# Moving a branch's key-value step behind the first denominators, with single weight loads and paired last heads, in a gated linear-attention kernel

## The chip, the cores and the metric

The kernel runs on one core of a Trainium2 chip. The metric is device time in microseconds (us) of one execution. Before the change it was 190.77 us (median of three runs, 190.71 to 191.03). A run's time is some 1.3 us longer than the span that the profile shows (for instance 191.05 against 189.7 in the profiled run of the kernel before), so spans are compared with spans and times with times.

Two sorts of numbers are used below. Times and ratios come from timed rounds. Everything inside a run comes from one profiled execution of each kernel.

## The reference, cut to what matters

Two linear-attention blocks, A and B, read the same x (2048 x 640) with their own weights, and a gate mixes them.

```python
x = A_x                                             # 1 x 2048 x 640, bf16
g = sigmoid((x * gate_w).sum(-1, keepdims=True))
def block(x, wqkv, wo):                             # H = 32 heads, Dh = 20
    q, k, v = split(x @ wqkv)
    phi = lambda t: where(t > 0, t + 1, exp(t)) + 1e-6
    pq, pk = phi(q), phi(k)
    kv  = einsum("bhsd,bhse->bhde", pk, v)          # 20 x 20 for each head
    z   = pk.sum over s
    num = einsum("bhqd,bhde->bhqe", pq, kv)
    den = einsum("bhqd,bhd->bhq", pq, z) + 1e-6
    return merge_heads(num / den) @ wo
out = g * block(x, A_wqkv, A_wo) + (1 - g) * block(x, B_wqkv, B_wo)
```

## The kernel before

The kernel never forms v for all positions. It forms G = phi(k)ᵀx, multiplies it by wv to get the kv of every head, and folds kv into wo: W' = blockdiag(kv) @ wo, 640 x 640 for each branch. The output is then (phi(q) / den) @ W' for A and for B, mixed by the gate.

A list scheduler inside the kernel receives operations in program order, each with an engine, an estimated duration and the buffers it reads and writes. It decides their order on each engine by simulated start time, and among operations that could start within 20 ns of each other by priority, which is program order. TensorE runs, in order: keys of A and B, the G products, the queries in blocks 0 to 3 (ten query units for each block, each five matmuls of 512 columns), and the finals, the matmuls that give the output. The denominators of two blocks are computed together. Their reciprocals, called the factor below, go through DRAM to come back in the layout of the queries (`RX`), and VectorE multiplies the queries by them.

A query unit also costs ScalarE an exponential, and VectorE two operations. The second of these is a max-add that reads the PSUM bank, and only then is the bank free for a later matmul.

```python
        def q_unit(X, b, k):
            # ... five matmuls into one PSUM bank (tile) ...
            # ACT : ek = exp(tile)
            # DVE : ek = min(ek, 1) + EPS
            # DVE : PQ[X][:, k, block b] = max(tile, 0) + ek        ("max-add", frees the bank)
```

The key-value step of a branch (`m_unit`) is a run of small matmuls, tiled to 64 columns of the array, two of them side by side. The last two heads have no partner and run one at a time. VectorE then copies the results into `MB` under a block-diagonal mask: two large masks (60 x 300) and a small one (40 x 40).

```python
        def m_unit(X):
            tile = _Tile(1)
            last = XS.index(X)
            def steps():
                r = []
                for q in range(6):
                    w = 12 if q < 5 else 8
                    for j in range(NC):
                        for g in (0, 1) if q < 5 else (last,):        # the last heads: one side only
                            at = D * j + 120 * q + 60 * g * (q < 5)
                            r.append((PS[64 * g : 64 * g + 64, ...], WV[X][:, at : at + 64], GT[X][...], j == 0, j == NC - 1, (0, 64 * g)))
                return r
            mms("m%s" % X, steps, [("GT", X, k) for k in range(NC)] + [("WV", X), ("WVP", X)], [(tile,)], 25 * 75 + 400)
            for q0, q1, g, w in ((0, 5, 0, 12), (0, 5, 1, 12), (5, 6, last, 8)):
                # ... DVE: MB[...] = PS[...] * mask ...
```

Six W' units follow (`wp_unit`: two matmuls of 320 columns, evicted to `WS`). `WS` is stored to DRAM and read back in another row order into `WPA` or `WPB` (`wp_store`, `wp_rows`). The finals of a branch need those rows.

```python
        def queries(b):
            for X in XS:
                for k in range(NC):
                    q_unit(X, b, k)
                    q = 5 * (X == "B") + k - WPLAG                    # WPLAG = 2
                    if b == 1 and 0 <= q < 6:
                        wp_unit("B", (q - 1) % 6)                     # the six W' units of B lie in block 1
                        if q == 0:
                            wp_rows("A")
        # ...
        queries(0)
        m_unit("B")
        queries(1)
        wp_store("B")
        wp_rows("B")
        d01 = dens(0)             # denominators of blocks 0 and 1: tiled to 32 columns
        scale_q(0, d01, 2)        # DVE: reciprocal; factor through DRAM; DVE: multiply the queries
        queries(2)
        queries(3)
        scale_q(1, d01, 2)
        d23 = dens(2)
        finals(0)
        # ... scale_q and finals of the other blocks ...
```

At the start, the key weights of A come in single chunks of 128 rows on two issuing queues, SP and ScalarE. Those of B come in three loads of one, two and two chunks, all on SP.

```python
        load_x("SP", 0);  load_wk("ACT", 0);  load_x("SP", 1);  load_wk("ACT", 1)
        load_wk("SP", 2); load_wk("ACT", 3);  load_wk("SP", 4)
        for c0, c1 in ((0, 1), (1, 3), (3, 5)):
            dma("SP", "wkB%d" % c0, WK["B"][:, c0:c1, :], weights("B", D, c0, c1), ...)
```

## Time and profile before

| | before |
|---|---|
| time, median | 190.77 us |
| span in the profile | 189.7 us |
| TensorE busy | 98% |
| VectorE busy | 69% |
| first 512-column matmul (end of the start) | 11.30 us |
| from there to the end ("body") | 178.44 us |

The page of the kernel before opens with the span and the busy time of each engine (share of the span, number of instructions). Its fourth part gives the chain of work that ended last.

```profile
span 189.7 us, 3209 instructions
...
PE 186.3 (98%) x1289; PEld 124.0 (65%) x1289; DVE 130.1 (69%) x275; ACT 76.4 (40%) x129; POOL 8.2 (4%) x14
...
PE 94%; DMA 3%; SPq 1%; DVE 0%; issue 0%; DVEq 0%
```

TensorE (PE) is the chain for 94% of the span, so a microsecond taken off PE counts, and so does a microsecond in which PE is made to wait. The 3% of DMA is the weight load at the start.

The table of stretches of the kernel before gives the busy time of each engine in a window. The first window is block 1 of the queries, the second blocks 2 and 3 after the denominators.

```profile
core 0: us, PE busy (x) PEld busy (x) DVE busy (x) ACT busy (x) POOL busy (x), PEclk, DMA share, GB/s
...
107.30:122.00 14.70, 14.70 (x77) 8.54 (x76) 12.72 (x26) 10.14 (x17) 0.00 (x0) 1.00 0.33 99
...
124.50:147.00 22.50, 22.50 (x119) 12.81 (x121) 22.13 (x45) 11.62 (x20) 0.00 (x0) 1.00 0.27 84
```

VectorE (DVE) has 2 us to spare in block 1 (12.72 of 14.70), where B's masks lie now. In blocks 2 and 3 it has almost none (22.13 of 22.50). An average over the whole span (69%) hides this.

The timeline of the kernel before, cut to the operations that the change moves (start, duration, engine, line, operation, count, and in brackets the idle time before it with its releaser). L383 is the helper that records every matmul, so matmuls are told apart by their tiles:

```profile
9.39 2.94 PE L383 MATMUL ps<-WK,XT 128*128 128x320 bf16 x18 [0.24 <-DMA WK<-in_B_wqkv_dram]
...
106.20 1.13 PE L383 MATMUL ps<-GTB,WVB 128*64 128x60 bf16 x55
...
107.36 1.02 DVE L647 TENSOR_TENSOR MB<-ps,CB 60x300 bf16<-60x300 f32 x1
...
117.30 0.44 PE L383 MATMUL ps<-WOB,MB 124*120 124x320 bf16 x2
...
118.72 0.34 SPq L372 DMA_DIRECT2D wrowsB<-WS  x1
...
123.72 0.35 SPq L372 DMA_DIRECT2D WPB<-wrowsB  x1
123.81 1.75 DVE L793 RECIPROCAL RC<-DN 128x256 bf16<-128x256 f32 x1
```

The wait at 9.39 us is the last that PE has. The key-value step of B runs at 106.20 us, its first large mask at 107.36, its last W' unit at 117.30. The rows are stored at 118.72, and their load is issued at 123.72 and lands at 127.91 (read from the trace). The first final of B uses them at 144.00.

### The profile page before, as it was taken

Reading aid. Unit: us, or ns where it says so; the run is one execution under the profiler, and the core shown is the slowest. Engines: PE = TensorE matmul, PEld = TensorE weight load, DVE = VectorE, ACT = ScalarE, POOL = GpSimd, SP = SyncE. Lnnn points to the kernel's source line nnn. Section 1 sums busy time; section 2 is a strip of 40 time slices with the busy share of each in tenths; the row PEclk is TensorE's granted clock in tenths of the full one; section 3 lists DMA queues with packets and bytes.
Section 4 is the critical chain, followed back from the end, with each engine's and each line's share of the span. In section 5 each row is a group of like instructions: output and inputs, shape, how many; then the busy total and the mean of one; then the engine's idle time right before and its main releaser. Section 6 shows DMA issues by size and latency. Waiting matters only on the chain.

```text
span 189.7 us, 3209 instructions
## 1 busy us (share of the span) xinstructions
PE 186.3 (98%) x1289; PEld 124.0 (65%) x1289; DVE 130.1 (69%) x275; ACT 76.4 (40%) x129; POOL 8.2 (4%) x14
## 2 busy tenths in 40 slices
PE   8999999999999999999999999999999999999995
PEld 3565555555788888888855666455556677777774
DVE  1398989898600009996179997899999959833324
ACT  2255555555311112203255478565553522331332
POOL 8900000000000000000000000000000000000000
DMA  6999699991011111112144004665000173211212
GB/s 184 282 229 202 183 381 371 352 241 43 0 35 38 35 35 38 35 35 38 35 86 111 5 22 173 165 223 171 0 0 3 43 228 92 97 66 46 73 69 69
DMA packets 31936, 21.49 MB, mean 113 GB/s; under 512 B 16818, under 2 KB 31666, under 8 KB 31922
## 3 DMA queue, kind: packets, MB, share of 16 engines
q1 hardware_dynamic: 31490, 20.80, 39.4%
q10 hardware_dynamic: 432, 0.49, 0.8%
q8 instruction: 10, 0.16, 0.4%
q14 instruction: 4, 0.03, 0.1%
HBM read 12.05 MB, written 5.31 MB: 91 GB/s over the span
## 4 chain that ended last, share of the span: by engine, by line
PE 94%; DMA 3%; SPq 1%; DVE 0%; issue 0%; DVEq 0%
PE ps L383 94%; DMA WK<-in_B_wqkv_dram 3%; SPq L372 1%; DVE OL L862 0%; DVEq L276 0%
## 5 line engine op out<-in xcount | busy, mean ns | idle before, releaser
L383 PE MATMUL ps<-WK,XT 128*128 128x512 bf16 (+2 forms) x250 | 44.1, 337 | 0.4 <-DMA WK<-in_B_wqkv_dram 0.2
L383 PE MATMUL ps<-XN,FE 128*128 128x320 bf16 x320 | 44.3, 300 | 0.0
L383 PEld LDWEIGHTS ps<-XN,FE 128*128 128x128 bf16 x320 | 37.5, 117 | 6.0
L383 PEld LDWEIGHTS ps<-WK,XT 128*128 128x128 bf16 x250 | 24.0, 98 | 20.2 <-DMA WK<-in_B_wqkv_dram 1.1
L743 ACT ACTIVATE EK<-ps 128x512 bf16<-128x512 f32 x40 | 23.9, 597 | 18.4 <-PE ps L383 17.4
L563 ACT ACTIVATE EK<-ps 128x512 bf16<-128x512 f32 (+1 forms) x42 | 21.4, 526 | 16.2 <-PE ps L383 16.2
L752 DVE SCALAR_TENSOR_TENSOR FE<-ps,EK 128x512 bf16<-128x512 f32 x40 | 26.8, 688 | 0.7
L856 ACT ACTIVATE TS<-ps,GA 128x640 f32<-128x640 f32 (+2 forms) x18 | 13.1, 735 | 29.3 <-PE ps L383 29.3
L383 PE MATMUL ps<-WPB,FE 128*128 128x320 bf16 (+1 forms) x165 | 24.5, 295 | 0.0
L383 PE MATMUL ps<-WPA,FE 128*128 128x320 bf16 (+1 forms) x165 | 24.5, 295 | 0.0
L573 DVE SCALAR_TENSOR_TENSOR FE<-ps,EK 128x512 bf16<-128x512 f32 (+1 forms) x42 | 23.9, 597 | 0.5
L862 DVE SCALAR_TENSOR_TENSOR OS<-ps,GA,TS 128x640 bf16<-128x640 f32 x15 | 13.0, 870 | 15.2 <-PE ps L383 15.2
L383 PE MATMUL ps<-XT,WQA 128*128 128x512 bf16 x100 | 22.8, 380 | 0.0
L383 PE MATMUL ps<-XT,WQB 128*128 128x512 bf16 x100 | 22.7, 379 | 0.0
L600 ACT ACTIVATE GS<-ps 128x640 bf16<-128x640 f32 x10 | 7.0, 704 | 37.0 <-PE ps L383 37.0
L383 PEld LDWEIGHTS ps<-WPA,FE 128*128 128x128 bf16 x165 | 16.0, 98 | 6.2
L383 PEld LDWEIGHTS ps<-WPB,FE 128*128 128x128 bf16 x165 | 15.8, 98 | 6.2 <-ACT TS L856 0.4
L383 PEld LDWEIGHTS ps<-XT,WQB 128*128 128x128 bf16 x100 | 11.7, 117 | 9.2
L383 PEld LDWEIGHTS ps<-XT,WQA 128*128 128x128 bf16 x100 | 11.6, 118 | 9.4 <-issue 0.4
L705 DVE SCALAR_TENSOR_TENSOR GP<-XN,GWB 128x640 bf16<-128x640 bf16 x16 | 13.3, 828 | 4.1 <-PE ps L383 3.6
L567 DVE TENSOR_SCALAR EK<-EK 128x512 bf16<-128x512 bf16 (+1 forms) x42 | 11.4, 272 | 3.1
L811 DVE TENSOR_TENSOR FE<-FE,RX 128x1280 bf16<-128x1280 bf16 (+1 forms) x20 | 12.6, 686 | 0.9 <-DMA RX<-factor 0.9
(52 smaller groups left out, 80.8 us busy)
## 6 DMA issues: line engine op xcount, KB each, us to landing
out_dram<-OS SPq DMA_DIRECT2D x15, 160.0 KB, 1.8
XN<-in_A_x_dram SPq DMA_DIRECT2D x3, 640.0 KB, 8.4
factor<-RC SPq DMA_DIRECT2D x4, 256.0 KB, 2.6
RX<-factor SPq DMA_DIRECT2D x4, 256.0 KB, 3.0
WVA<-in_A_wqkv_dram SPq DMA_DIRECT2D x1, 800.0 KB, 10.8
WQA<-in_A_wqkv_dram SPq DMA_DIRECT2D x1, 800.0 KB, 12.2
WVB<-in_B_wqkv_dram SPq DMA_DIRECT2D x1, 800.0 KB, 11.2
WQB<-in_B_wqkv_dram SPq DMA_DIRECT2D x1, 800.0 KB, 12.2
```

Of the source, the lines that this page charges most:

```text
L372: ins = e.dma_start(dst() if callable(dst) else dst, src() if callable(src) else src, transpose=transpose)
L383: ins = pe.matmul(o, l, r, start=a, stop=z, tile_position=tp, skip_group_check=True)
L563: "ACT", lambda e, ps=ps, ek=ek: e.activation(ek(), ps(), ACT.Exp), _act_ns(n), reads=[(tile,)], writes=[(es,)],
L567: "DVE", lambda e, ek=ek: e.tensor_scalar(ek(), ek(), 1.0, EPS, op0=ALU.min, op1=ALU.add), _dve_ns(n, 4),
L573: return e.scalar_tensor_tensor(out=out, in0=two(ps()), scalar=0.0, in1=two(ek()), op0=ALU.max, op1=ALU.add)
L600: "ACT", lambda e: e.activation(GS[:, k, :].rearrange("p (h f) -> p h f", f=HALF), pair(tile, HALF), ACT.Copy),
L705: lambda e, t=t: e.scalar_tensor_tensor(out=GP[:, :], in0=XN[:, t, 0:D], scalar=1.0, in1=GWB[:, :], op0=ALU.mult, op1=ALU.mult, accum_out= ...
L743: "ACT", lambda e: e.activation(ek(), PS[:, tile.banks[0], :], ACT.Exp), _act_ns(512), reads=[(tile,)],
L752: lambda e: e.scalar_tensor_tensor(out=dst, in0=PS[:, tile.banks[0], :], scalar=0.0, in1=ek(), op0=ALU.max, op1=ALU.add),
L811: return e.tensor_tensor(out=v, in0=v, in1=RX[:, xs.slot, 512 * x + w * j : 512 * x + w * j + w].unsqueeze(1).to_broadcast([128, NC, w]), ...
L856: "ACT", lambda e: e.activation(t_ap(), acc(), ACT.Copy, scale=GA[:, 0, t : t + 1]), _act_ns(hi - lo),
L862: lambda e: e.scalar_tensor_tensor(out=o_ap(), in0=acc(), scalar=GA[:, 1, t : t + 1], in1=t_ap(), op0=ALU.mult, op1=ALU.add),
```

## The change

The intent is to take a few tenths of a microsecond off TensorE. The last heads of A and B run side by side. The key-value step goes directly behind the denominators, so one change of the array's tiling mode falls away. The weights of B arrive in single chunks, so the last bytes hold up fewer matmuls. The W' units of B then have to move from block 1 into blocks 2 and 3.

```diff
-WPLAG = 2
+WPAT = (25, 26, 27, 29, 30, 31)
@@ loads @@
-        for c0, c1 in ((0, 1), (1, 3), (3, 5)):
-            dma(
-                "SP", "wkB%d" % c0, WK["B"][:, c0:c1, :], weights("B", D, c0, c1), ...
-            )
+        for c in range(NC):
+            load_wk(("SP", "ACT")[c % 2], "B", c)
@@ m_unit (cut) @@
-        def m_unit(X):
-            tile = _Tile(1)
+        def m_unit(X, after=None):
+            tiles = [_Tile(1)] + [_Tile(1)] * (X == "B")
             def steps():
+                r = [step(X, tiles[0], q, g, j) for q in range(5) for j in range(NC) for g in (0, 1)]
+                if X == "B":
+                    r += [step(Y, tiles[1 - g], 5, g, j) for j in range(NC) for g, Y in enumerate(XS)]
                 return r
+            parts = [(0, 0, 5, 0, 12), (0, 0, 5, 1, 12)]
+            if X == "B":
+                parts = [(1, 5, 6, 0, 8), (0, 5, 6, 1, 8)] + parts      # two small masks, then two large ones
@@ dens / scale_q (cut): the two copies of the denominators move from scale_q into dens @@
@@ queries @@
-                    q = 5 * (X == "B") + k - WPLAG
-                    if b == 1 and 0 <= q < 6:
-                        wp_unit("B", (q - 1) % 6)
-                        if q == 0:
+                    p = 10 * b + 5 * (X == "B") + k
+                    if p in WPAT:
+                        i = WPAT.index(p)
+                        wp_unit("B", (i - 1) % 6)
+                        if i == 0:
                             wp_rows("A")
+                        if i == 5:
+                            wp_store("B")
+                            wp_rows("B")
@@ order at the end @@
         queries(0)
-        m_unit("B")
         queries(1)
-        wp_store("B")
-        wp_rows("B")
-        d01 = dens(0)
-        scale_q(0, d01, 2)
+        d0, d1 = dens(0)
+        m_unit("B", den[0])
         queries(2)
+        scale_q(0, d0, 2)
         queries(3)
-        scale_q(1, d01, 2)
-        d23 = dens(2)
+        scale_q(1, d1, 2)
+        d2, d3 = dens(2)
```

A number in `WPAT` counts query units from the first of block 0, so 25 is the sixth unit of block 2 and 31 the second of block 3.

More of the change, by code (lines that the diff above doesn't have):

```diff
@@ L409, in load_x, with load_wk @@
             dma(eng, "xn%d" % t, XN[:, t, 0:D], xin[128 * t : 128 * t + 128, :], writes=[("XN", t)], us=0.25)
-        def load_wk(eng, c):
-            dma(eng, "wkA%d" % c, WK["A"][:, c, :], weights("A", D, c, c + 1)[:, 0, :], writes=[("WK", "A", c)], us=0.25)
+        def load_wk(eng, X, c):
+            dma(eng, "wk%s%d" % (X, c), WK[X][:, c, :], weights(X, D, c, c + 1)[:, 0, :], writes=[("WK", X, c)], us=0.25)
         load_x("SP", 0)
-        load_wk("ACT", 0)
+        load_wk("ACT", "A", 0)
         load_x("SP", 1)
-        load_wk("ACT", 1)
-        load_wk("SP", 2)
-        load_wk("ACT", 3)
-        load_wk("SP", 4)
-        for c0, c1 in ((0, 1), (1, 3), (3, 5)):
-            dma(
-                "SP", "wkB%d" % c0, WK["B"][:, c0:c1, :], weights("B", D, c0, c1), writes=[("WK", "B", c) for c in range(c0, c1)],
-                us=0.55 * (c1 - c0),
-            )
+        load_wk("ACT", "A", 1)
+        load_wk("SP", "A", 2)
+        load_wk("ACT", "A", 3)
+        load_wk("SP", "A", 4)
+        for c in range(NC):
+            load_wk(("SP", "ACT")[c % 2], "B", c)
         for t0, t1 in ((2, 4), (4, 8), (8, 12), (12, 16)):
@@ L620, in zbd @@
             )
-        def m_unit(X):
-            tile = _Tile(1)
-            last = XS.index(X)
-            def steps():
-                r = []
-                for q in range(6):
-                    w = 12 if q < 5 else 8
-                    for j in range(NC):
-                        for g in (0, 1) if q < 5 else (last,):
-                            at = D * j + 120 * q + 60 * g * (q < 5)
-                            r.append((
-                                PS[64 * g : 64 * g + 64, tile.banks[0], 60 * q : 60 * q + NC * w], WV[X][:, at : at + 64],
-                                GT[X][:, j, :, 24 * q + 12 * g * (q < 5) : 24 * q + 12 * g * (q < 5) + w], j == 0, j == NC - 1, (0, 64 * g),
-                            ))
-                return r
-            mms("m%s" % X, steps, [("GT", X, k) for k in range(NC)] + [("WV", X), ("WVP", X)], [(tile,)], 25 * 75 + 400)
-            for q0, q1, g, w in ((0, 5, 0, 12), (0, 5, 1, 12), (5, 6, last, 8)):
+        den = {}
@@ new lines, in m_unit, with step @@
+        def m_unit(X, after=None):
+            tiles = [_Tile(1)] + [_Tile(1)] * (X == "B")
+            def step(Y, tile, q, g, j):
+                w, lo = (12, 12 * g) if q < 5 else (8, 0)
+                at = D * j + 120 * q + DH * lo // 4
+                return (
+                    PS[64 * g : 64 * g + 64, tile.banks[0], 60 * q : 60 * q + NC * w], WV[Y][:, at : at + 64],
+                    GT[Y][:, j, :, 24 * q + lo : 24 * q + lo + w], j == 0, j == NC - 1, (0, 64 * g),
+                )
+            def steps():
+                r = [step(X, tiles[0], q, g, j) for q in range(5) for j in range(NC) for g in (0, 1)]
+                if X == "B":
+                    r += [step(Y, tiles[1 - g], 5, g, j) for j in range(NC) for g, Y in enumerate(XS)]
+                return r
+            ys = XS if X == "B" else ("A",)
+            mms(
+                "m%s" % X, steps, [("GT", Y, k) for Y in ys for k in range(NC)] + [("WV", Y) for Y in ys] + [("WVP", Y) for Y in ys],
+                [(t,) for t in tiles], (len(tiles) + 9) * 190 + 240, after=after,
+            )
+            parts = [(0, 0, 5, 0, 12), (0, 0, 5, 1, 12)]
+            if X == "B":
+                parts = [(1, 5, 6, 0, 8), (0, 5, 6, 1, 8)] + parts
+            for i, q0, q1, g, w in parts:
@@ L642, in m_unit, with mask @@
                 n = DH * (w // 4)
-                def mask(e, q0=q0, q1=q1, g=g, w=w, n=n):
+                def mask(e, i=i, q0=q0, q1=q1, g=g, w=w, n=n):
                     p0 = 64 * g
@@ L648, in mask @@
                         out=MB[p0 : p0 + n, q0:q1, 60 * g : 60 * g + n].rearrange("p q (i k) -> p q k i", k=NC),
-                        in0=PS[p0 : p0 + n, tile.banks[0], 60 * q0 : 60 * q0 + n * (q1 - q0)].rearrange("p (q k i) -> p q k i", k=NC, i=w),
+                        in0=PS[p0 : p0 + n, tiles[i].banks[0], 60 * q0 : 60 * q0 + n * (q1 - q0)].rearrange(
+                            "p (q k i) -> p q k i", k=NC, i=w
+                        ),
                         in1=m.unsqueeze(1).to_broadcast([n, q1 - q0, NC, w]), op=ALU.mult,
@@ L653, in m_unit @@
                 sch.op(
-                    "DVE", mask, _dve_ns(n * (q1 - q0)), reads=[(tile,), ("CB",)], writes=[("M", q) for q in range(q0, q1)],
+                    "DVE", mask, _dve_ns(n * (q1 - q0)), reads=[(tiles[i],), ("CB",)], writes=[("M", q) for q in range(q0, q1)],
                     name="mm%s" % X,
@@ L760, in dens, with steps @@
             dtile = _Tile(1)
-            def den():
+            def steps():
                 r = []
@@ L773, in den, with scale_q @@
                 return r
-            mms(
-                "den%d" % b0, den, [("ZBD", X) for X in XS] + [("PQ", X, k, b) for X in XS for k in range(NC) for b in (b0, b0 + 1)],
+            den[b0] = mms(
+                "den%d" % b0, steps, [("ZBD", X) for X in XS] + [("PQ", X, k, b) for X in XS for k in range(NC) for b in (b0, b0 + 1)],
                 [(dtile,)], 5 * 540,
             )
-            return dtile
-        def scale_q(b, dtile, pieces):
-            ds = _Tile(1, ring["dn"])
-            lo = 256 * (b % 2)
-            sch.op(
-                "ACT",
-                lambda e: e.activation(DN[:, ds.slot, :], PS[:, dtile.banks[0], lo : lo + 256], ACT.Identity, bias=EP[:, 0:1]), _act_ns(256),
-                reads=[(dtile,), ("EP",)], writes=[(ds,)], name="dn%d" % b,
-            )
+            ds = []
+            for b in (b0, b0 + 1):
+                d = _Tile(1, ring["dn"])
+                ds.append(d)
+                sch.op(
+                    "ACT",
+                    lambda e, d=d, lo=256 * (b - b0): e.activation(
+                        DN[:, d.slot, :], PS[:, dtile.banks[0], lo : lo + 256], ACT.Identity, bias=EP[:, 0:1]
+                    ),
+                    _act_ns(256), reads=[(dtile,), ("EP",)], writes=[(d,)], name="dn%d" % b,
+                )
+            return ds
+        def scale_q(b, ds, pieces):
             def rec(e):
@@ L936, in bass_gated_mix__linear_attn_block__linear_attn_block__prompt_kernel @@
         queries(0)
-        m_unit("B")
         queries(1)
-        wp_store("B")
-        wp_rows("B")
-        d01 = dens(0)
-        scale_q(0, d01, 2)
+        d0, d1 = dens(0)
+        m_unit("B", den[0])
         queries(2)
+        scale_q(0, d0, 2)
         queries(3)
-        scale_q(1, d01, 2)
-        d23 = dens(2)
+        scale_q(1, d1, 2)
+        d2, d3 = dens(2)
         finals(0)
-        scale_q(2, d23, 2)
+        scale_q(2, d2, 2)
         finals(1)
-        scale_q(3, d23, 4)
+        scale_q(3, d3, 4)
         finals(2)
```

## The prediction

> **What bounds the kernel now.** The page shows TensorE (PE) busy 98% of 189.7 us; the chain of waits is PE for 94%, with 3% for the load of the second wk at the start. From 9.39 us to the last matmul PE never waits. But VectorE (DVE) is as full where blocks 2 and 3 of the queries run: the table of stretches gives DVE 22.13 of 22.50 us from 124.5 to 147.0, and only 12.7 of 14.7 us in block 1 before it.
>
> **What the change does, on PE (starts read in the timeline).**
> 1. Start. The last four matmuls of the first B tile wait until 9.39 us for a two-chunk load. With single chunks only two should wait for the last chunk: estimate 0.27 us saved (two matmuls at 136 ns), if the last byte lands when it did.
> 2. Last heads in pairs. An unpaired 64x40 matmul takes 32 ns, a pair too. The A step loses its five: 0.16 us saved.
> 3. B key-value step behind the denominators. Entering a column-tiled stretch costs 309 ns instead of 216, leaving it about 0.1 us. The Trainium skill (TensorEngine Tiling (Array Packing), Key Properties) says that changing the tiling mode drains the array; the trace agrees with these 0.1 us. One such change fewer: 0.1 to 0.2 us saved.
>
> Sum: about 0.6 us less PE work.
>
> **What it moves.** The four B masks (two of 1.02 us, two of 0.29) and the six W' units leave block 1, where DVE had room, and go behind the two reciprocals (1.75 us each) in block 2, where it has none. From the first denominator matmul (T), with durations of the trace: denominators copied T+1.8, reciprocals and small masks to about T+5.4, the two large masks with one query step between them to about T+8.4. PE's own work to the first W' unit that needs them (denominators 1.1, key-value 1.1, five queries at 1.08, one unit 0.27) ends at about T+7.9. So PE waits about 0.5 us there, then about 0.6 us for the next query unit, whose bank frees only when DVE has caught up (that query's max-add, about T+9.2 to 9.6). These waits swallow saving 3.
>
> **Second new wait.** In the trace, 10.6 us pass from the last W' unit of B to its rows being back (store 4.9, load 4.2, both by DMA). Before, the rows were back 14 us before need. After, only eight query units and the first A half of the final lie between: 8 x 1.08 + 1.36 + 0.27 = 10.3 us; ScalarE also evicts a query first. Estimate: PE waits 0.5 us at the first final of B.
>
> **Prediction.** -0.6 + 1.1 + 0.5 = about +0.9 us; PE is the chain, so all of it counts: 191.5 us, 8 in 10 between 190.3 and 192.5. Faster by over 2%: 0.01; within 2%: 0.97; slower: 0.02.
>
> **What would show it.** Right: the first 512-column matmuls start about 0.3 us earlier; the denominators start near 118.8 us, not 122.0; the waits list PE on DVE masks or max-adds around 126 to 128 us, and PE on the DMA of the B rows near 143; finals begin near 143, not 142.6. Wrong: no PE idle in blocks 2 and 3.
>
> **What would make it wrong.** If consecutive masks overlap more on DVE than I took, the first waits halve. If the rows come back faster on the quiet queue, the second wait vanishes: then 190.2. If the extra loads on ScalarE's queue delay the first branch's chunks, step 1 gives nothing.

## The result, and the profile after

| | before | after |
|---|---|---|
| time, median of six runs (range) | 190.74 us (190.50 to 191.07) | 192.83 us (192.47 to 193.68) |
| ratio after to before (95% interval) | | 1.0116 (1.0092 to 1.0141) |
| span in the profile | 189.7 us | 192.0 us |
| first 512-column matmul (after: see below) | 11.30 us | 11.60 us |
| body (span less the line above) | 178.44 us | 180.44 us |

The kernel got slower by 2.1 us. That is within 2%, as predicted, but the time lies above the predicted range of 190.3 to 192.5 us.

The page of the kernel after, the same parts:

```profile
span 192.0 us, 3199 instructions
...
PE 186.4 (97%) x1279; PEld 124.0 (65%) x1289; DVE 130.7 (68%) x275; ACT 76.5 (40%) x129; POOL 8.1 (4%) x14
...
PE 83%; DMA 8%; DVE 5%; SPq 1%; ACT 1%; issue 1%; DVEq 0%; ACTq 0%
```

PE falls from 94% of the chain to 83%; DMA and VectorE take its place. The counts need care. PE shows 1279 matmuls and 1289 weight loads. Ten matmul records are missing from this trace, so a missing 216 ns is taken for a wait only where the weight load is late too. The record of the first 512-column matmul is among the missing ones in every trace but that of the kernel before; its start is put one ordinary distance (216 ns) before the second's, where its weight load stands too. The same holds for busy time: it did not fall although work was taken away. All PE waits of this document are therefore measured from the starts of successive matmuls in the trace, less the ordinary distance (216 ns for 512 columns, 136 ns for 320). The waits view gives somewhat less, because the ends of matmuls are modelled.

What TensorE waited for in the kernel after (total us, times, longest us):

```profile
...
PE ps L383 <- DVE FE L760: 0.7, 1, 0.7
PE ps L383 <- DVE MB L653: 0.6, 1, 0.6
PE ps L383 <- DMA WPB<-wrowsB: 0.4, 1, 0.4
...
```

These are the new waits that the prediction named: a mask (MB), a max-add (FE), and the rows of B (WPB). By the starts of matmuls they are 0.72, 0.87 and 0.61 us.

The table of stretches of the kernel after, for the window in which masks, W' units and queries of blocks 2 and 3 now lie together:

```profile
122.00:144.30 22.30, 20.93 (x99) 11.71 (x100) 22.11 (x43) 13.83 (x23) 0.00 (x0) 1.00 0.49 142
```

VectorE is full again (22.11 of 22.30), and now PE is not (20.93). How the 1.6 us of the first two waits arise is seen in the timeline of VectorE in the kernel after, from the denominators on. They started at 119.30 us.

```profile
121.12 1.75 DVE L804 RECIPROCAL RC<-DN 128x256 bf16<-128x256 f32 x1
122.79 0.20 DVE L653 TENSOR_TENSOR MB<-ps,CB 40x40 bf16<-40x40 f32 x1
122.84 1.73 DVE L804 RECIPROCAL RC<-DN 128x256 bf16<-128x256 f32 x1
124.61 0.29 DVE L653 TENSOR_TENSOR MB<-ps,CB 40x40 bf16<-40x40 f32 x1
124.92 0.29 DVE L755 TENSOR_SCALAR EK<-EK 128x512 bf16<-128x512 bf16 x1
125.25 1.02 DVE L653 TENSOR_TENSOR MB<-ps,CB 60x300 bf16<-60x300 f32 x1
126.03 0.75 DVE L760 SCALAR_TENSOR_TENSOR FE<-ps,EK 128x512 bf16<-128x512 f32 x1
126.81 1.02 DVE L653 TENSOR_TENSOR MB<-ps,CB 60x300 bf16<-60x300 f32 x1
127.86 0.49 DVE L755 TENSOR_SCALAR EK<-EK 128x512 bf16<-128x512 bf16 x2
128.39 1.29 DVE L760 SCALAR_TENSOR_TENSOR FE<-ps,EK 128x512 bf16<-128x512 f32 x2
```

The scheduler put the second reciprocal between the small masks, and the large ones came last. The last large mask ends at 127.83, and the timeline of PE shows the two consequences:

```profile
127.98 0.45 PE L383 MATMUL ps<-WOB,MB 124*120 124x320 bf16 x2 [0.56 <-DVE MB L653]
...
129.14 0.41 PE L383 MATMUL ps<-XT,WQB 128*128 128x512 bf16 x1 [0.70 <-DVE FE L760]
```

The first W' unit that needs the large masks could have started at 127.26. The query unit behind it needs a bank that a max-add frees at about 129.09.

The chain of the kernel after shows the third wait, with the round trip of the rows (start, duration, what):

```profile
136.19 0.61 ACT WS L690
136.81 4.91 DMA wrowsB<-WS
...
141.79 4.43 DMA WPB<-wrowsB
146.22 0.05 issue
146.27 43.27 PE ps L383 x335
```

What answers to the wait at 9.39 us of before, in the timeline of the weight loads of PE (PEld) at the start:

```profile
6.69 0.39 PEld L383 LDWEIGHTS ps<-WK,XT 128*128 128x128 bf16 x4 [0.47 <-DMA WK<-in_A_wqkv_dram]
...
7.53 0.93 PEld L383 LDWEIGHTS ps<-WK,XT 128*128 128x128 bf16 x8 [0.45 <-DMA WK<-in_A_wqkv_dram]
...
9.41 2.50 PEld L383 LDWEIGHTS ps<-WK,XT 128*128 128x128 bf16 x19 [0.41 <-DMA WK<-in_B_wqkv_dram]
```

PE now waits twice for weights of A, where it waited once before (0.4 us). The two waits end with the third and fourth of A's five chunks, which landed (arrived in SBUF) at 6.65 and 7.48 us, against 5.69 and 6.71 before. The last chunk of A landed at 7.71 us against 7.10 before, and the last of B at 9.75 against 9.35.

The bookkeeping of the body is then: +0.72 +0.87 (mask and query unit) +0.61 (rows) −0.15 (five unpaired matmuls fewer) −0.13 (one change of mode fewer) = +1.92 us, of 2.00 measured (180.44 less 178.44). The start adds 0.29 in this pair of profiles.

### The profile page after: what moved, and what is told of

Read it like the earlier page. It is cut to its first block, busy times and chain, and to the rows that moved or that the text cites. A ratio compares the mean times of both kernels' runs of the same rounds, so it can differ in the third digit from the quotient of the medians.

```text
span 192.0 us, 3199 instructions
## 1 busy us (share of the span) xinstructions
PE 186.4 (97%) x1279; PEld 124.0 (65%) x1289; DVE 130.7 (68%) x275; ACT 76.5 (40%) x129; POOL 8.1 (4%) x14
## 3 DMA queue, kind: packets, MB, share of 16 engines
HBM read 12.05 MB, written 5.31 MB: 90 GB/s over the span
## 4 chain that ended last, share of the span: by engine, by line
PE 83%; DMA 8%; DVE 5%; SPq 1%; ACT 1%; issue 1%; DVEq 0%; ACTq 0%
PE ps L383 83%; DMA WK<-in_B_wqkv_dram 3%; DMA wrowsB<-WS 3%; DMA WPB<-wrowsB 2%; DVE RC L804 2%; DVE MB L653 1%; SPq L372 1%; DVE FE L760 1%; ACT EK L751 1%; DVE EK L755 1%; DVE OL L873 0%; ACT WS L690 0%; DVEq L276 0%; SPq L274 0%; ACTq L276 0%
## 5 line engine op out<-in xcount | busy, mean ns | idle before, releaser
L383 PE MATMUL ps<-XT,WQA 128*128 128x512 bf16 x95 | 21.8, 379 | 0.4 <-issue 0.2
```

The source lines that it names most:

```text
L383: ins = pe.matmul(o, l, r, start=a, stop=z, tile_position=tp, skip_group_check=True)
```

## The experiments

Fourteen kernels ran, in four groups. Each was correct, with six timed runs (four for the repeat of the changed kernel). The theory is that the loss has three parts: the order of work on VectorE, the late rows, and the start's loads. Its rivals are that VectorE's load itself makes PE wait, whatever the order; that the paired heads or the tiling cost time; and that the start only varies from run to run and the loads don't matter.

Landing times and starts are from one profile each:

| kernel | loads of B's weights | last chunk of A lands | first 512-column matmul | body | ratio to before (95%) |
|---|---|---|---|---|---|
| before | old | 7.10 | 11.30 | 178.44 | |
| after | two queues | 7.71 | 11.60 | 180.44 | 1.0116 |
| start_two_queues | two queues | 8.65 | 12.15 | 178.46 | 1.0011 (0.9986 to 1.0035) |
| start_one_queue | single, one queue | 6.89 | 11.03 | 178.46 | 0.9994 (0.9970 to 1.0018) |
| old_loads | old | 6.52 | 10.78 | 180.07 | 1.0088 (1.0067 to 1.0110) |
| late_recip | old | 6.71 | 11.12 | 179.04 | 1.0029 (1.0008 to 1.0050) |
| early_w | old | 6.98 | 11.20 | 179.80 | 1.0068 (1.0052 to 1.0083) |
| all_three | old | 6.61 | 10.70 | 178.89 | 1.0067 (1.0035 to 1.0099) |
| all_three_one_queue | single, one queue | 7.78 | 11.56 | 179.68 | 1.0038 (1.0007 to 1.0069) |
| after_again | two queues | 7.79 | 11.83 | 180.38 | 1.0129 (1.0113 to 1.0146) |
| order_and_room | old | 6.20 | 10.44 | 178.68 | 1.0011 (0.9994 to 1.0029) |
| order_and_room_two | two queues | 8.58 | 12.05 | 178.71 | 1.0045 (1.0026 to 1.0065) |
| order_and_room_one | single, one queue | 6.32 | 10.62 | 178.70 | 0.9986 (0.9971 to 1.0000) |
| pairs_only | old | 6.23 | 10.92 | 178.28 | 0.9982 (0.9966 to 0.9998) |
| pairs_one_queue | single, one queue | 7.34 | 11.03 | 178.31 | 1.0007 (0.9989 to 1.0025) |
| pairs_two_queues | two queues | 8.07 | 11.69 | 178.31 | 1.0020 (0.9994 to 1.0045) |

### The start alone: the change's loads, and the same chunks on one queue

Both edits are made to the kernel before.

```diff
 # start_two_queues
+        for c in range(NC):
+            dma(("SP", "ACT")[c % 2], "wkB%d" % c, WK["B"][:, c, :], weights("B", D, c, c + 1)[:, 0, :], ...)
 # start_one_queue
+        for c in range(NC):
+            dma("SP", "wkB%d" % c, WK["B"][:, c, :], weights("B", D, c, c + 1)[:, 0, :], ...)
```

> The kernel before, with only the start of the change: the five wk chunks of the second branch one by one, alternately on SyncE's and ScalarE's queue. Theory (the extra loads on ScalarE's queue take DMA time from the first branch's chunks, so every chunk lands later): 0.2 to 0.4 us slower than before, first 512-column matmul near 11.6 us against 11.30, and a new wait of TensorE for a chunk of the FIRST branch's wk longer than the 0.2 us it has before. Rival 1, the prediction's step 1 (single chunks save two matmuls' wait): 0.27 us faster, first 512-column matmul near 11.0. Rival 2 (the start of the changed kernel's profile was chance of one run): no difference, within 0.1 us.

> The kernel before, with the five chunks of the second branch one by one, but all on SyncE's queue behind the first branch's. Theory (it is the second queue that does the harm, not the smaller loads): the first branch's chunks land as before (last near 7.1 us), the second's in order, and the start is 0.1 to 0.3 us faster than before, unless the x transposes, whose issue slides 0.9 us, come too late for the first 512-column matmul. Rival (single chunks themselves move less per us): as slow as with two queues, 0.2 to 0.4 us slower than before.

Measured: 190.98 us with two queues, 190.66 with one, 190.85 before, and all three intervals overlap. The bodies are equal (178.46 and 178.46 against 178.44), so the loads change the start and nothing else. In the profile the two differ clearly. This is PE's wait in start_two_queues:

```profile
PEld ps L383 <- DMA WK<-in_A_wqkv_dram: 1.6, 1, 1.6
...
PE ps L383 <- DMA WK<-in_A_wqkv_dram: 1.2, 1, 1.2
```

The wait ends at 7.79 us, with the third of the first branch's five chunks, which landed at 7.75 us against 6.37 with one queue. The last chunk is late too (8.65 against 6.89), but PE did not wait for it. Late chunks of A are where the prediction said this step would go wrong. The slowdown of 0.2 to 0.4 us expected of start_two_queues is not shown by the timed runs (0.13 us over before). The timed difference between the two on this chip is only 0.3 us and not settled by itself; the last two groups below repeat it.

### The change with the old loads

```diff
 # old_loads: the kernel after, with before's three loads of B
-        for c in range(NC):
-            load_wk(("SP", "ACT")[c % 2], "B", c)
+        for c0, c1 in ((0, 1), (1, 3), (3, 5)):
+            dma("SP", "wkB%d" % c0, WK["B"][:, c0:c1, :], weights("B", D, c0, c1), ...)
```

> The changed kernel with the loads of before at the start. If the start costs 0.3 us by itself and nothing later hides it, this is 0.3 us faster than the changed kernel, so near 192.5 us, 1.8 us slower than before; TensorE's waits at the large masks (0.7), at the query unit behind (0.9) and at the second branch's rows (0.6) stay as they are. If the start does not matter, it equals the changed kernel, 192.8.

Measured: 192.47 us, ratio 1.0088. The body is 180.07 us, with the two VectorE waits unchanged (0.74 and 0.87 us) and the rows' wait at 0.25. Most of the loss is thus in the body: 1.6 of 2.1 us remain with the loads put back.

### The second reciprocal behind block 2

The reciprocal of block 1's denominators is needed late. Here it may only start after the last max-add of block 2, so it can no longer slip between the masks.

```diff
 # late_recip: old_loads, and
-        def scale_q(b, ds, pieces):
+        def scale_q(b, ds, pieces, after=None):
-            sch.op("DVE", rec, 1740, ..., name="rc%d" % b)
+            sch.op("DVE", rec, 1740, ..., name="rc%d" % b, after=after)
         queries(2)
+        done2 = next(o for o in reversed(sch.ops) if o.name == "sqB24")
-        scale_q(1, d1, 2)
+        scale_q(1, d1, 2, done2)
```

> The changed kernel with the loads of before and one more edit: the reciprocal of block 1 (1.75 us on VectorE) waits for the last query of block 2, so that it no longer stands among the masks. VectorE's total work is unchanged. Theory (the masks come late because reciprocals stand ahead of them in VectorE's order): the waits at the large masks and at the query unit behind, 1.6 us together, shrink to under 0.3 us, and only the 0.6 us wait for the second branch's rows stays: about 191.0 us, 1.5 us under the same kernel without this edit. Rival (VectorE has too much work in blocks 2 and 3 whatever its order): TensorE's wait comes back a few units later, at a query unit of block 3 or at the first finals, and the gain is under 0.5 us.

Measured: 191.42 us, 1.05 less than old_loads in the same group, where 1.5 had been expected. Its timeline, cut to VectorE's reciprocal and masks and the W' unit that had waited:

```profile
120.64 1.75 DVE L807 RECIPROCAL RC<-DN 128x256 bf16<-128x256 f32 x1
...
122.31 0.52 DVE L656 TENSOR_TENSOR MB<-ps,CB 40x40 bf16<-40x40 f32 x2
...
123.34 1.02 DVE L656 TENSOR_TENSOR MB<-ps,CB 60x300 bf16<-60x300 f32 x1
...
124.91 1.03 DVE L656 TENSOR_TENSOR MB<-ps,CB 60x300 bf16<-60x300 f32 x1
...
126.78 0.44 PE L383 MATMUL ps<-WOB,MB 124*120 124x320 bf16 x2
...
127.05 1.27 PE L383 MATMUL ps<-XT,WQB 128*128 128x512 bf16 x5
```

No idle time stands before the last two lines: both waits, 1.59 us in the kernel after, are gone. The small masks follow each other, and the last large one ends 1.4 us earlier than in the kernel after, counted from the first 512-column matmul (125.94 − 11.12 = 114.82 us against 127.83 − 11.60 = 116.23). So it was the order on VectorE that made these two waits. What was not gained shows in its waits view:

```profile
PE ps L383 <- DMA WPB<-wrowsB: 0.7, 1, 0.7
```

Counted from the first 512-column matmul, PE is ready for the first final of B 1.6 us earlier than in old_loads, and the rows land only 1.1 us earlier: the wait grew from 0.25 to 0.86 us by starts. The store took 5.2 us here instead of 4.9, beside the store of block 1's factor (136.87 to 140.72 us), which the later reciprocal had moved onto the same stretch. A part of the gain was handed from one wait to the next.

### The W' units of B earlier

```diff
 # early_w: old_loads, and
-WPAT = (25, 26, 27, 29, 30, 31)
+WPAT = (22, 23, 24, 25, 26, 27)
```

> The changed kernel with the loads of before and the W' units of the second branch three query units earlier where the masks allow it (the last of them 11 query units ahead of the first final, not 8); VectorE's order at the masks unchanged. Theory (two independent waits): the 0.25 to 0.6 us wait of the first second-branch final for its rows goes, as they land about 2.5 us before need; the waits at the large masks and the query unit behind, 1.6 us, stay: about 192.1 us. Rival (the late masks are the one cause, and the rows' wait is only their echo): the rows' wait stays, because the masks still end where they ended.

Measured: 192.05 us, ratio 1.0068. The waits on VectorE in its profile:

```profile
PE ps L383 <- DVE FE L763: 0.7, 1, 0.7
PE ps L383 <- DVE MB L656: 0.6, 1, 0.6
```

They are those of old_loads (0.74 and 0.87 us by starts, in both), and no wait for the rows is left: they landed at 142.98 us, and the first final of B began at 145.27. The two kinds of wait are independent, and each has its own remedy.

### All remedies at once

```diff
 # all_three: old_loads with WPAT = (24, 25, 26, 27, 28, 29); block 0's reciprocal after the last mask,
 # block 1's after the last max-add of block 2, both with a priority to match.
 # all_three_one_queue: the same, with single chunks of B on SP
```

> The changed kernel with the loads of before, both reciprocals behind the masks (block 0's right behind the last mask, block 1's behind block 2's last query), and the W' units spread from the second query of the second branch in block 2 (the last 10 query units ahead of the first final). Theory (the change's own saving is real, 0.15 us for the pairs and 0.13 us for one change of tiling mode less, and everything else it costs lies in these three waits): no wait of TensorE over 0.1 us after the start, and 0.2 to 0.4 us FASTER than before, about 190.5 us. Rival (VectorE's load in blocks 2 and 3 must show up somewhere): at least 0.5 us of waits at query units of block 3 or the first finals, and not faster than before.

> The same with the second branch's wk chunks one by one on SyncE's queue alone. If the single chunks in one queue gain what the profile of that start alone suggests, 0.2 us under all_three, about 190.3 us; if the start is only chance from run to run, equal to it within 0.1 us.

Both expectations missed. all_three measured 192.03 us, scattered from 190.91 to 192.81, where 190.5 had been expected; all_three_one_queue 191.64 (190.34 to 192.56). The profiled execution of all_three was the fastest of its six (body 178.89), that of all_three_one_queue the slowest (179.68). But even the former had waits of 0.25 us at a W' unit and 0.35 us at a final, both for VectorE, where none over 0.1 us was expected: the rival named there held. Between the two bodies the clearest difference is in VectorE's first multiplication by the factor, first all_three, then all_three_one_queue:

```profile
130.92 0.82 DVE L825 TENSOR_TENSOR FE<-FE,RX 128x1280 bf16<-128x1280 bf16 x1 [0.55 <-DMA RX<-factor]
```

```profile
132.54 0.82 DVE L822 TENSOR_TENSOR FE<-FE,RX 128x1280 bf16<-128x1280 bf16 x1 [1.29 <-DMA RX<-factor]
```

Moving block 0's reciprocal behind the masks made its factor late, and VectorE stood still for it by 0.55 or 1.29 us. In all_three_one_queue PE then waited 0.41 and 0.69 us at finals. How much of the scatter of the timed runs comes from this wait is open: only these two executions were seen, and 0.86 of the 1.65 us between their spans lies in the start.

### The changed kernel once more

after_again is the changed kernel without an edit, in the second group.

> The changed kernel itself, unedited, beside the others on their chip: 192.5 to 193.0 us, 1.1% over before; the three waits of its first profile again, 0.7, 0.9 and 0.3 to 0.7 us. Its start scatters: first 512-column matmul between 11.3 and 12.2 us.

Measured: 193.15 us against 190.63 before, ratio 1.0129, just above the expected range; waits 0.74, 0.87 and 0.52 us, body 180.38. Result and bookkeeping repeat.

### Order and room, with three ways to load

Only the second reciprocal moves here, and less far, so block 0's factor stays early. The last W' unit is one query unit earlier. The intent that block 1's factor should keep clear of the store of B's rows failed: its load ran from 133.53 to 139.41 us, the store from 133.15 to 138.66, so the store again took long (5.5 us).

```diff
 # order_and_room: old_loads, and
+WPAT = (25, 26, 27, 28, 29, 30)
+        done2 = next(o for o in reversed(sch.ops) if o.name == "sqB20")      # the sixth query unit of block 2
+        scale_q(1, d1, 2, done2)                                             # with a priority to match
 # order_and_room_two: the same with the change's loads;  order_and_room_one: single chunks on SP alone
```

> The changed kernel with the loads of before; block 0's reciprocal where the change has it, the four masks right behind it, block 1's reciprocal only behind the sixth query unit of block 2, and the last W' unit 9 query units ahead of the first final, not 8. In all_three the later block 0 reciprocal put its factor loads behind other transfers, and VectorE waited for them; this should not happen here. Theory: waits at masks, at the query unit behind and at the second branch's rows all under 0.15 us; time 190.4 to 190.7 us, equal to before or up to 0.3 us faster (0.28 us of TensorE's work saved). Rival (VectorE's load must show): 0.5 us or more of waits at later query units or finals, and slower than before by as much.

> The same with the change's own loads at the start (single chunks, two queues). If the second queue costs time by itself: 0.3 to 0.8 us over order_and_room, and the last chunk of the first branch's wk lands after 7.4 us in its profile, against 6.2 to 7.1 with the loads of before. If the start is chance: equal within 0.15 us.

> The same with single chunks on SyncE's queue alone. If only the second queue harms: equal to order_and_room or up to 0.2 us faster. If single chunks harm by themselves: as slow as with two queues.

order_and_room measured 190.99 us (ratio 1.0011) with a body of 178.68, so 1.4 of old_loads' 1.6 us body loss is recovered. The time is above the 190.4 to 190.7 us expected. The waits at the masks are gone, and the rows land at 142.98 us, 0.1 us before PE could have used them (143.08). Two short waits remain. One is at a query unit:

```profile
130.87 1.03 PE L383 MATMUL ps<-XT,WQA 128*128 128x512 bf16 x4 [0.25 <-DVE EK L758]
```

It comes behind the moved reciprocal (128.27 to 130.0 us), and is 0.19 us by starts. The other, 0.30 us, is at the first final of B, which waits for a max-add to free its bank. (The profile names the rows' load there, but that had landed 0.4 us before the start; the max-add ended 0.15 us before it, at 143.24.) So the rival that blames VectorE's load is right for 0.5 us of waits: in this order too, VectorE has no room in this stretch. Its other half, slower than before by as much, the timed runs do not show (interval 0.9994 to 1.0029).

The loads, on this chip: 190.99 us with the old ones, 191.67 with the change's, 190.56 with single chunks on one queue. The intervals of the last two do not overlap (1.0026 to 1.0065 against 0.9971 to 1.0000), while the three bodies agree within 0.03 us (178.68, 178.71, 178.70). The second queue costs 1.1 us against one queue here, and all of it lies in the start: 12.05 against 10.62 us to the first 512-column matmul.

### The paired heads alone, with three ways to load

```diff
 # pairs_only: the kernel after, with the old loads, m_unit("B") and the W' units back in block 1
+WPAT = (12, 13, 14, 15, 16, 17)
         queries(0)
+        m_unit("B")
         queries(1)
         d0, d1 = dens(0)
-        m_unit("B", den[0])
 # pairs_one_queue: the same with single chunks on SP;  pairs_two_queues: with the change's loads
```

> The kernel before with only the paired last heads: the B key-value step and its W' units stay in block 1. Expected: the A step shorter by 0.15 us in its profile (five unpaired matmuls of 32 ns gone), the B step as long as before, no new wait of TensorE, time 0.1 to 0.2 us under before (which five rounds may not separate from nothing). If the masks, now four at B and two at A, cost TensorE something even in block 1: no gain.

> The kernel before with the paired last heads and the second branch's wk chunks one by one on SyncE's queue; B key-value step and W' units stay in block 1. Body (from the first 512-column matmul to the end) 178.3 us as in pairs_only; start 10.5 to 11.1 us: 190.2 to 190.5 us, 0.1 to 0.5 us under before.

> The same with two of the five chunks moved to ScalarE's queue, as the change has it. If the second queue is what costs at the start: 0.3 to 0.7 us over pairs_one_queue in the timed runs, last chunk of the first branch after 7.4 us in the profile. If its cost is chance: equal within 0.15 us.

pairs_only measured 190.48 us, ratio 0.9982 (0.9966 to 0.9998), and has no new wait. Its body is 178.28, that of the other two 178.31: 0.13 to 0.16 us below the kernel before in three traces, which is what five unpaired matmuls of 32 ns make. This is the best-founded gain of the change, and too small to be called a faster kernel; pairs_one_queue stands at 1.0007. order_and_room_one (0.9986, upper end at 1.0000) doesn't clearly beat the kernel before either.

Again the loads on two queues are the slowest of the three: 191.08 against 190.74 on one (same chip), with the last chunk of A at 8.07 against 7.34 us. By itself the interval of this pair does not settle it, and pairs_one_queue missed its expected 190.2 to 190.5 us.

## Why the prediction was wrong

It said 191.5 us with a range up to 192.5, and the median was 192.83. Its own terms summed to +1.0 us (it wrote "about +0.9", and then 191.5, which is only +0.7), so part of the distance was already in how the sum was taken to the final figure. Term by term:

| term | predicted | measured |
|---|---|---|
| 1. start, single chunks on two queues | −0.27 | +0.29 in this pair of profiles; +0.1 to +1.1 in timed comparisons |
| 2. last heads in pairs | −0.16 | −0.15 |
| 3. one change of tiling mode fewer | −0.1 to −0.2 | −0.13 |
| W' unit waits for the masks | +0.5 | +0.72 |
| next query unit waits for its bank | +0.6 | +0.87 |
| first final of B waits for the rows | +0.5 | +0.61 |
| not assigned | | +0.05 to 0.1 |

**The step that failed is step 1, in its sign.** From −0.27 to +0.29 it accounts for 0.56 us of the miss in this pair of profiles. It is not alone: the waits in blocks 2 and 3, right in kind, were put 0.49 us too low, and the rows' wait 0.11. The prediction took the start to be 0.27 us shorter "if the last byte lands when it did". It did not. With B's chunks 1 and 3 on ScalarE's queue, the last chunk of the first branch landed at 7.7 to 8.7 us in the five profiles with two queues, at 6.2 to 7.1 in the profiles with the old loads, and at 6.3 to 7.8 with single chunks on one queue. The first 512-column matmul came at 11.6 to 12.15 us, against 10.4 to 11.3 and 10.6 to 11.6. In time the second queue cost 0.3, 0.3 and 1.1 us against one queue (three comparisons within a chip), and 0.1 and 0.7 against the old loads; the changed kernel against old_loads gives 0.36, from different rounds. Of the comparisons with one queue only the last stands outside the intervals, but all point the same way, and the landings do too. (The ranges of the landings touch: 7.78 with one queue, 7.71 with two. The starts do not: all five with two queues, from 11.60 us, lie above all eleven others, up to 11.56. Which late chunk PE waits for differs: the third, fourth or fifth of A, and in four of the five also the first of B.) The prediction had listed this as what would make step 1 wrong ("the extra loads on ScalarE's queue delay the first branch's chunks"), and allowed for a gain of nothing, not for a loss.

The rival that the start only varies is half right. It does vary: seven profiles with the old loads spread over 0.9 us, and the 11.30 of the kernel before happens to be their latest, so the +0.29 of the first pair of profiles is small. The means are 10.92 us with the old loads (seven profiles), 11.06 with one queue (four) and 11.86 with two (five), a loss of 0.9 us in the profiles. The timed comparisons give 0.1 to 1.1. What the second queue costs in a typical run is therefore known in sign and not closely in size.

Single chunks as such do no harm, and show no clear gain either: 0.9994, 1.0007 and 0.9986 against before in kernels that have them on one queue.

The Trainium skill (Trainium Kernel Development and Optimization, Key Constraints) says that DMAs from several engines' queues "all run on the same 16 DMA engines and interleave", and that issuing from several engines only saves the sequencer's issue time. The first half fits the runs: in the kernel after, B's second chunk was issued at 2.15 us, right beside A's last (2.12), where the kernel before issues the first of B at 2.60; and A's last chunk was late. That the interleaving is the cause was not shown. What was shown is that the landings are late with the second queue and not with the chunk size. The second half understates it: here the second queue had a price, above.

**The waits in blocks 2 and 3 were right in kind and place, and put too low.** They were put at 1.1 us and measured 1.59. Several small terms add up. The denominators began at 119.30 us instead of 118.8; this is mostly the start and moves all the rest along, so it costs nothing by itself. The last large mask ended 8.53 us after them (8.4 was predicted), and PE started 0.15 us after the mask's end, which the prediction took as nothing. Then VectorE ran two of the queries' min-adds (0.49 us) ahead of the max-add that PE needed: that max-add ended 9.79 us after the start of the denominators, where 9.2 to 9.6 was predicted (one min-add, 0.29 us, and one max-add, 0.69 us, behind the predicted 8.4 would give 9.4, an estimate). The prediction had taken VectorE's order between masks and reciprocals as given. late_recip and order_and_room show that it was the thing to change: with the second reciprocal elsewhere the same work runs without these waits, though others come (the rows in late_recip, two short ones in order_and_room).

**Why the scheduler chose that order** can be argued from its code, and the order itself is seen in the timeline. Each mask depends on the one before, through the shared PSUM tile and the shared `MB`, with 180 ns of modelled latency; in that gap the reciprocal would look ready first. The model also takes a large mask for 300 / 0.96 + 68 = 380 ns, and the trace shows 1.02 us. No run corrected the model, so how much either matters stays open.

**The rows' wait was right** (0.5 predicted, 0.61 in the profile, 0.52 in the repeat, 0.25 with the old loads). The store took 4.9 and the load 4.4 us, where 4.9 and 4.2 had been read from the kernel before. early_w showed that it can be removed while the mask waits stay, late_recip that it grows when they go.

**Steps 2 and 3 were right.** pairs_only shows step 2 by itself; step 3 is read from starts in the traces, and no run isolates it. An unpaired 64 x 40 matmul takes 32 ns, hardly more than a pair takes (31.5 ns). The Trainium skill (TensorE: Matmul & The Clock Gate, "Wait — 56ns, not 53.3ns?") says that the distance between starts never falls below about 25 ns. The trace agrees only in part: pairs of 60 columns and of 40 follow each other at the same 31.5 to 32 ns, so the columns do not set this distance, but the two matmuls of a pair start 3 to 4 ns apart. Whether the 32 ns come from that floor was not tested. The change of mode costs PE 93 ns on entering (309 instead of 216 ns), 86 + 33 ns on leaving 64-column tiling (spread over two matmuls) and 95 + 32 ns on leaving 32-column tiling. The last, 0.13 us, is what falls away; the skill (TensorEngine Tiling (Array Packing), Key Properties) says that changing the mode drains the array, and these extra times agree with it.

One point of the reading was right, and with it the direction of the whole: the 69% of VectorE's busy share was no room at all in the stretch into which 2.6 us of masks were moved (two of 1.02 us and two of 0.29).

## What to carry to other kernels

Before moving work, look at how full each engine is in the stretch it moves to, not over the whole span; a saving of 0.13 us in one engine's mode changes cost 1.6 us of waits, because VectorE was full there and the order in which it served masks and reciprocals decided when TensorE went on. When loads are on the critical path at the start, split them if that helps, but don't let a later branch's chunks travel beside those needed first: count what is in flight on all queues. And when one wait is taken away, look at the next one in the chain before adding up the gain; here the rows' round trip took back 0.6 us of the 1.6.

## What the Trainium skill lacked or had wrong

- Trainium Kernel Development and Optimization, Key Constraints: it says that issuing DMAs from several engines only saves issue time. Here the same five chunks alternately on two queues were slower than on one by 0.3, 0.3 and 1.1 us in three comparisons (only the last outside the intervals), and in the profiles the chunks needed first landed later (the last of A at 8.65, 8.07 and 8.58 us against 6.89, 7.34 and 6.32). That the queues interleave is said there; that this can delay the loads needed first is not.
- TensorEngine Tiling (Array Packing), Key Properties: it says that changing the mode drains the array, without a size. The trace shows 93 ns on entering 64-column tiling from the full array, 93 ns between 32-column and 64-column tiling, and 86 + 33 or 95 + 32 ns on leaving 64 or 32 columns. So changing the tile size costs what entering does.
- TensorE: Matmul & The Clock Gate, "Wait — 56ns, not 53.3ns?": the floor between starts is given as about 25 ns. For 64-column tiles the trace shows 31.5 ns from pair to pair and 32 ns between lone ones, and 3 to 4 ns between the two of a pair, so that floor does not hold between matmuls on different tiles.
- VectorE: DVE Perf Modes: no duration for a reciprocal was found there. 128 x 256 elements (fp32 to bf16) took 1.75 us here, 128 x 32 (fp32 to fp32) took 0.35 us; from these two an estimate is 6.2 ns for each further element of a row.
- The same page ("The TRN2 errata") gives (N + 151) / 0.96 ns for a tensor-tensor addition of N fp32 elements, found exact there for N = 512 and 2048, which as an estimate would be 0.47 us for N = 300. The 60 x 300 mask, a multiplication with strided bf16 output, a repeated operand and its input in PSUM, which the page does not say the formula covers, took 1.02 us. Which of these costs the time was not tested.
